# One tile of left rows for a block instead of one for a step, and dense operands turned one unit a step in the forward chain

## The chip, the cores and the metric

The kernel runs on one core of a Trainium2 chip. The time is device time of one execution in microseconds; it is given as the median of several runs. Besides these runs there is one profiled execution, from which all views of the profile come. TensorE is called PE in the profile (its weight loads PEld), VectorE DVE, ScalarE ACT, GpSimd POOL and SyncE SP. "DMA share" is the mean busy share of the core's 16 DMA engines.

## The reference

Two functions of the same layer-normed input are added to x, and the whole is differentiated: the outputs are the result and the gradients of all ten inputs for a given grad_out, 11 arrays in bf16.

```python
xn = _layernorm(x)                     # x: 1 x 2048 x 512
return x + _A_ref(xn, mem0, Wq, Wk, Wv, Wo, 32) + _B_ref(xn, w1, b1, w2, b2)

def _A_ref(...):                       # 32 heads of 128, M = 8 memory rows
    mem = mem0                         # 8 x 512
    for s in range(64):                # segments of 32 rows, one after the other
        h = concatenate([mem, xs])     # 40 rows
        q, k, v = h @ Wq, h @ Wk, h @ Wv
        scores = where(mask, q k^T * scale, -1e9)    # idx_q < 8, or causal
        o = softmax(scores) @ v @ Wo
        mem = o[:8]; outs.append(o[8:])

def _B_ref(...):                       # F = 1792
    r = relu(x @ w1 + b1)
    return r * r @ w2 + b2
```

The memory rows make the 64 segments a chain, forwards and, for the gradients, backwards. A memory row attends to all 40 keys of its segment.

## The kernel before

**Rows.** Of a segment's 40 rows (8 of memory, 32 of x) a step of the chain handles 32: the memory and the first 24 of x. They are called the main rows. The last 8 rows of a segment, the *left rows*, take no part in making the next memory as queries, but their keys and values do, and these hang on x alone. Their q, k and v are projected ahead for a whole block and kept in DRAM in S_NL[b][:, t], t = 0, 1, 2 for q, k, v. A block is four segments, j = 0 to 3, so a block has 32 left rows for each of four groups of heads: the 128 partitions are 4 groups of 32 rows, and left row m of segment j lies at row 8j + m of its group. Each group has eight heads, which stand side by side in 1024 columns (GW).

**Stages**, in order of time: the dense function B with its backward part to 215 us; the first left rows to 250; the forward chain to about 1110; its tail; the left-back stage from 1143 to about 1386 (16 iterations, one per block: the gradients of left queries, and beside them the dense weight gradients); the backward chain to about 2330 (64 steps, from the last segment to the first); the weight gradients of A (L1639) to the end.

**Order.** In both chains the instructions are issued in an order written by hand. F_ORDER and B_ORDER list names of small pieces of work in four strings, one for each step of a block ("slots"); a plus sign behind a name means one step (or, for names with "L.", one block of the left thread) later. `play` walks through it. Each engine then executes its own instructions in that order. In the backward chain slot 0 is segment j = 3, slot 3 is j = 0. Plain transfers named `dma` and all DMA transposes sit on one queue, SyncE's; it is in order, so an entry that waits holds back all behind it. `pdma` is GpSimd's queue.

**Attention in a step.** `scores` (L467) computes q k^T into PSUM, the softmax writes the probabilities to E [128, 8 heads, KW = 64 columns] (all zero at the start): columns 0 to 31 the main keys, 32 to 39 the left keys. `turn` (L480) transposes 32x32 blocks on DVE, so that for each head ET has main keys (`[.., 0, :]`) and left keys (`[.., 1, :]`) on the partitions. `outer` (L620) then multiplies, for each head and group, main values by the first and left values by the second, both into the same PSUM tile f_pp. Since the second block has only 8 rows with keys, the left values of the step must lie at partitions 0 to 7 of each group. So `left_of_step` (L636 to 639) loads them for every step by four DMAs of 16 KB, into f_vLs forwards (values, the name `ld`; two buffers) and into b_kLs backwards (keys, the name `ldk`, L1336; one buffer), where `qp` multiplies the transposed score gradients gST by them. The backward chain's further loads of a step (qN, kN, P, the transposed values vl with `vtr`) come from S_A, where the forward chain stored them (soV L956, soN L957, soP L958). The left thread of the forward chain has also a tile of a whole block's left values, VL (one buffer, loaded by L.lv), as well as vM, the memory rows' values.

**Stores of gradients.** The backward chain collects the gradients of q, k, v in G4 for a block; in slot 0 six stores of 512 KB (L1238, names L.vo1, L.vo0, L.qo0, L.ko0, L.ko1, L.qo1) take them to S_GB. The casts (evictions) `ve`, `ke` and `qe` of the next block write the same G4.

**Dense weight gradients.** They need the hidden activations and their gradients with rows on partitions, while the dense stage stored both turned: S_AT and S_GH1T, [4 row blocks, 1792, 512]. In the left-back stage `chunk` (L1085) loads 256 of the 1792 columns of one of them by four DMA transposes of 256 KB each to wB, one chunk an iteration ahead, 14 chunks; `product` (L1101, L1106) multiplies it by the other operand wA, which stays in SBUF. The iteration's other loads (transposed left values vTL, vTM, P, kM, kL) are on the same queue ahead of the chunk (`load`).

**The names in short.** f_vLs, b_kLs: a step's left values and keys. VL: a block's left values. S_AT, S_GH1T: dense operands as stored. wB: a chunk, turned. E, P, gS: probabilities and score gradients. kT, vT: transposed keys and values of a step, copied together from main and left.

Of the kernel before, what the change touches and what calls it, by code (L numbers as in the profile page):

```python
# [8 lines left out]
ALU = mybir.AluOpType  # L9
# [17 lines left out]
def kernel(  # L27
# [96 lines left out]
    S_GH1T = dram.tile([NRB, F, RB], BF16, name="S_GH1T")  # L124

# [47 lines left out]
    def masks(pool, temp):  # L173
# [11 lines left out]
        for g in range(HG):  # L185
            sl = slice(32 * g, 32 * g + 32)

            keep(maskA[sl, :, M:SEG], [[0, KM], [-1, XS]], -M, 1)
            nc.gpsimd.memset(maskA[32 * g:32 * g + M, :, :], 0.0)

            keep(maskl1[sl, 0], [[-M, SPB], [0, M]], 0, 1)
            keep(maskl1[sl, 0], [[M, SPB], [0, M]], M - 1, -1)
            keep(maskl1[sl, 1], [[-M, SPB], [-1, M]], 0, 1)
            keep(maskl1[sl, 1], [[-M, SPB], [0, M]], 0, 1)
            keep(maskl1[sl, 1], [[M, SPB], [0, M]], M - 1, -1)
# [11 lines left out]
    with sb("p1b", 2) as p1b, sb("p1", 1) as p1:  # L207
# [90 lines left out]
        for rb in range(NRB):  # L298
# [26 lines left out]
            else:  # L325
# [6 lines left out]
                XL0, X0 = (smp.tile([P, DC, P], BF16, name=n) for n in ("XL0", "X0"))  # L332
# [161 lines left out]

    C01, C23 = slice(0, 2), slice(2, 4)
# [67 lines left out]
    def ds_ops(o, p, n, sc, Pb, gS, sm):  # L563
# [14 lines left out]
        def d4():  # L578
            nc.vector.scalar_tensor_tensor(out=gS()[:, HALF[p], 0:n], in0=t[0][:], scalar=scale,  # L579
                                           in1=Pb()[:, HALF[p], :], op0=ALU.mult, op1=ALU.mult)  # L580
        o["d1%d" % p], o["d2%d" % p], o["d3%d" % p], o["d4%d" % p] = d1, d2, d3, d4

    def soft_ops(o, p, n, sc, E, st, sm, tag, pre=""):
# [21 lines left out]
        def pmf():  # L605
            e = nc.vector if ENGS[pre + "pm%d" % p] is vcp else nc.gpsimd
            e.tensor_tensor(out=E()[:, HALF[p], 0:n], in0=st[p][:], in1=bc(ss[1], n), op=ALU.mult)
# [3 lines left out]
    def outer(pp, h, jobs, base=0):  # L611

        for k in range(4):
            for i, (c0, w, ends, m, N_, X) in enumerate(jobs):
                for g in range(HG):
                    o = pp[g // 2][:, g % 2, base + k * c0:base + k * c0 + w]
                    if ends:
                        o = o.rearrange("p (a n) -> p a n", a=2)[:, :, 0:M]
# [16 lines left out]

    def left_of_step(eng, dst, b, j, t):  # L636

        for g in range(HG):
            eng(dst[32 * g:32 * g + M], S_NL[b, 32 * g + M * j:32 * g + M * j + M, t, :])
# [14 lines left out]
    def play(order, n, steps, lefts, step, blk, done=None):  # L654
# [20 lines left out]

    F_ORDER = (
# [3 lines left out]
        "ta+++ Ha+++ L.u2 L.mx0+ L.t1 soV+++ tb+++ L.X2 Hb+++",  # L680
# [5 lines left out]
        "rb+++ L.oa0+ ta+++ Ha+++ tb+++ Hb+++",  # L686
# [4 lines left out]
        "tu1+++ w1+++ L.lq++ oa1+++ ob1+++ g0+++ g1+++ soN++ ra+++ rb+++ ta+++ Ha+++ tb+++ L.otr+ Hb+++",  # L691
# [986 lines left out]
```

## Time and profile before

| what | value |
|---|---|
| runs | 2919.82, 2922.25, 2928.49 us; median 2922.25 |
| profiled execution: own time, span, granted clock | 2915.0 us, 2913.1 us, 0.971 |
| forward chain, 250 to 1110 us | 860 us, PE busy 810 |
| left-back stage, 1143 to 1386 us | 243 us, PE busy 193 |
| backward chain, 1386 to 2330 us | 944 us, PE busy 870 |
| wB transposes (L1085) in that stage | 56, four for each of 14 chunks |
| f_vLs and b_kLs loads | 256 each of 16 KB |

A stage of the profile is read from its window: the length, the busy time and number of instructions of each engine, the clock that TensorE was granted, the share of the DMA engines and the GB/s they moved. A row of waits reads "engine, its operation and line, `<-` what ended the wait", then the total in us, the number of times and the longest. A row that ends in "issue" is idle time in which the profile shows no event that the engine waited for. The granted clock is 1.00 at full speed.

### The profile page before, as it was taken

Reading aid. Unit: us, or ns where it says so; the run is one execution under the profiler, and the core shown is the slowest. Engines: PE = TensorE matmul, PEld = TensorE weight load, DVE = VectorE, ACT = ScalarE, POOL = GpSimd, SP = SyncE. Lnnn points to the kernel's source line nnn. Section 1 sums busy time; section 2 is a strip of 40 time slices with the busy share of each in tenths; the row PEclk is TensorE's granted clock in tenths of the full one; section 3 lists DMA queues with packets and bytes.
Section 4 is the critical chain, followed back from the end, with each engine's and each line's share of the span. In section 5 each row is a group of like instructions: output and inputs, shape, how many; then the busy total and the mean of one; then the engine's idle time right before and its main releaser. Section 6 shows DMA issues by size and latency. Waiting matters only on the chain.

```text
span 2913.1 us, 115280 instructions
## 1 busy us (share of the span) xinstructions
PE 2702.2 (93%) x51252; PEld 1450.9 (50%) x51252; DVE 1277.8 (44%) x3754; ACT 1001.7 (34%) x2330; POOL 660.6 (23%) x1278
## 2 busy tenths in 40 slices
PE   7997999999999887888898999999999999999999
PEld 3444555555555555355454554455555444444444
DVE  4533566666665654343454545454445401100000
ACT  2313444444444445232333333333333301111111
POOL 1000000000000001122333433343334324332221
PEclk9998999999999998998899999999999999999999
DMA  9766477667676668999666687677767799999993
GB/s 250 259 207 164 138 184 189 184 188 182 180 192 166 170 156 201 227 225 213 148 167 164 179 220 173 172 180 211 184 170 181 223 273 224 220 209 237 217 210 71
DMA packets 835429, 561.50 MB, mean 193 GB/s; under 512 B 642177, under 2 KB 727698, under 8 KB 833394
## 3 DMA queue, kind: packets, MB, share of 16 engines
q1 hardware_dynamic: 794018, 431.40, 64.6%
q0 software_dynamic: 40912, 122.73, 14.0%
q8 instruction: 402, 6.59, 0.9%
q14 instruction: 97, 0.79, 0.1%
HBM read 174.47 MB, written 234.11 MB: 140 GB/s over the span
## 4 chain that ended last, share of the span: by engine, by line
PE 42%; DMA 7%; issue 2%; DVE 1%; SPq 1%; POOL 0%; ACT 0%; ACTq 0%; DVEq 0%; POOLq 0%
PE ps_gw L1639 17%; PE ps_gR L490 11%; PE ps_proj L422 3%; PE b_pp L620 3%; PE ps_RL L1251 3%; DMA b_kLs<-S_NL 2%; PE b_T L525 1%; PE ps_tr L164 1%; DMA gn<-S_OL 1%; DMA b_qN<-S_A 1%; PE ps_R L490 1%; DMA S_GM<-b_GN 1%; PE b_pp L1383 1%; PE ps_sc L467 1%; DMA b_GN<-GT 0%
## 5 line engine op out<-in xcount | busy, mean ns | idle before, releaser
L1639 PE MATMUL ps_gw<-gn,HNc 128*128 128x512 bf16 x1920 | 416.8, 379 | 0.0
L1639 PEld LDWEIGHTS <-HNc 128*128 128x128 bf16 x1920 | 187.9, 98 | 223.6
L404 ACT CAST f_N<-ps_proj 128x512 bf16<-128x512 f32 x320 | 183.9, 581 | 199.4 <-PE ps_proj L422 192.6
L1572 ACT CAST wt<-ps_gw 128x512 bf16<-128x512 f32 x128 | 74.0, 588 | 451.3 <-PE ps_gw L1639 412.0
L422 PEld LDWEIGHTS <-X 128*32 128x32 bf16 x6144 | 152.6, 96 | 143.1 <-DVE X L534 21.9
L1555 DVE TENSOR_TENSOR gx<-ps_rows,gb 128x512 f32<-128x512 f32 x16 | 11.1, 692 | 426.4 <-PE ps_rows L1553 426.4
L895 POOL COPY kM<-f_kT 128x256 bf16<-128x256 bf16 x64 | 25.8, 403 | 736.0 <-DVE f_kT L407 562.2
L490 PE MATMUL ps_gR<-Wv,gv 128*32 128x512 bf16 x2048 | 145.0, 404 | 6.9 <-issue 6.9
L1639 PE MATMUL ps_gw<-GOc,gn 128*128 128x512 bf16 x640 | 141.0, 383 | 10.2 <-ACT wt L1572 8.7
L490 PE MATMUL ps_gR<-Wk,gk 128*32 128x512 bf16 (+1 forms) x2048 | 141.1, 387 | 1.3 <-ACT gk L404 0.8
L490 PE MATMUL ps_R<-Wo,OT 128*32 128x256 bf16 x4096 | 135.6, 289 | 1.1 <-DVE OT L407 1.1
L422 PE MATMUL ps_proj<-Wq,X 128*32 128x512 bf16 x2048 | 134.7, 380 | 0.1
L404 ACT CAST gk<-b_pp 128x256 bf16<-128x256 f32 x192 | 70.7, 379 | 184.0 <-PE b_pp L620 116.1
L422 PE MATMUL ps_proj<-Wk,X 128*32 128x512 bf16 x2048 | 130.9, 380 | 0.8
L422 PE MATMUL ps_proj<-Wv,X 128*32 128x512 bf16 x2048 | 131.3, 382 | 0.0
L404 ACT CAST gON<-ps_proj 128x512 bf16<-128x512 f32 x128 | 75.0, 586 | 157.4 <-PE ps_proj L422 157.4
L490 PE MATMUL ps_gR<-Wq,gq 128*32 128x512 bf16 (+1 forms) x2048 | 122.8, 348 | 6.8 <-issue 6.8
L422 PE MATMUL ps_proj<-Wo,GT 128*32 128x512 bf16 x2048 | 123.3, 382 | 3.7 <-DVE GT L1296 3.6
L1573 POOL DMA_DIRECT2D out_dram<-wt x120 | 65.0, 543 | 255.7 <-ACT wt L1572 241.0
L1332 POOL COPY PD<-b_P 32x320 bf16<-32x320 bf16 x256 | 115.3, 450 | 8.0
L490 PEld LDWEIGHTS <-OT 128*32 128x32 bf16 x4096 | 109.3, 102 | 9.9 <-DVE OT L407 1.3
L1327 POOL DMA_DIRECT2D b_P<-S_A x63 | 33.9, 538 | 349.9 <-DVE gS L579 115.6
(276 smaller groups left out, 5256.7 us busy)
## 6 DMA issues: line engine op xcount, KB each, us to landing
S_A<-f_N SPq DMA_DIRECT2D x64, 512.0 KB
out_dram<-wt POOLq DMA_DIRECT2D x134, 128.0 KB, 4.9
S_A<-f_N SPq DMA_DIRECT2D x64, 256.0 KB
S_GB<-gv SPq DMA_DIRECT2D x32, 512.0 KB
S_GB<-gq SPq DMA_DIRECT2D x32, 512.0 KB
S_GB<-gk SPq DMA_DIRECT2D x32, 512.0 KB
b_kN<-S_A POOLq DMA_DIRECT2D x63, 256.0 KB, 3.9
b_qN<-S_A POOLq DMA_DIRECT2D x63, 256.0 KB, 4.1
```

The lines of the kernel that those rows point to most:

```text
L164: nc.tensor.transpose(ps_ap, in_ap, ident[base:base + k, base:base + k])
L404: nc.scalar.copy(out, in_)
L422: nc.tensor.matmul(o, lhsT=hT[:, dc, :], rhs=x, start=(dc == 0), stop=(dc == DC - 1), tile_position=(0, 32 * g))
L467: nc.tensor.matmul(sc3[32 * g:32 * g + 32, k, c:c + n], lhsT=qT[:, 4 * h + k, g, :], rhs=kT[:, 4 * h + k, g, :], start=(mask is None), sto ...
L490: nc.tensor.matmul(R[32 * g:32 * g + 32, 0:(cs.stop - cs.start) * P].rearrange("p (a b) -> p a b", b=P), lhsT=XT(k, g), rhs=x[:, cs, :], s ...
L620: nc.tensor.matmul(o, lhsT=N_[32 * g:32 * g + m, kk * P:(kk + 1) * P], rhs=X(kk)[32 * g:32 * g + m], start=(i == 0), stop=(i == len(jobs) ...
L1251: nc.tensor.matmul(ps["R", i][32 * g:32 * g + 32, :].rearrange("p (a b) -> p a b", b=P), lhsT=B_[n][:, k, g, :], rhs=W(g * KH + k), start= ...
L1327: q(tile_of("P", [P, KH, KW])[:], rows[:, 3 * GW:AC].rearrange("p (k n) -> p k n", k=KH))
L1332: nc.gpsimd.tensor_copy(PD[32 * g:32 * g + 32, g], C["P"][32 * g:32 * g + 32, :, 0:L])
L1572: nc.scalar.copy(wt[:], ps[:])
L1573: eng(dst, wt[:])
L1639: nc.tensor.matmul(ps[:], lhsT=l(rc), rhs=r(rc), start=(n == 0), stop=(n == RC_ALL - 1))
```

## The change

1. *Order of rows.* In kT, vT, in E, P and gS and in all that is evicted from products with them, the 8 left rows come first (columns 0 to 7) and the main rows after (`MAIN = slice(8, 40)`). E and gS use the last columns of their 64: left 24 to 31, main 32 to 63; 0 to 23 stay zero. Masks, score operands and products are swapped to match.
2. *Left rows of a block in one tile.* `turn` gets j and reads overlapping windows of E: for every head 32 columns that start at 24 - 8j, and 32 that start at 32. So the left keys of segment j come to rows 8j to 8j + 7, with zeros before them, and `outer` multiplies rows 0 to 8 + 8j of the block's tile. Forwards that tile is VL, now with two buffers and loaded in slot 0 one block ahead. Backwards it is a new tile kNL (one buffer), loaded once a block in two halves of 128 KB, ldk1 and ldk0, on SyncE's queue in slot 0. f_vLs, b_kLs and `left_of_step` are gone.
3. *Dense operands turned ahead.* In steps 4 to 59 of the forward chain each step transposes one unit of 256 KB (`aw`, a DMA transpose to the tile `box`, which uses the space of XL0 and X0) and stores it plainly (`as`) to the new DRAM arrays S_AN and S_GH1N, both on SyncE's queue. `chunk` in the left-back stage is then one plain load of 1 MB.
4. *Orders.* F_ORDER and B_ORDER are cut in other places between slots, which alone moves nothing on PE, DVE and ACT: the sequence of their operations is the one before, but for which of the two operands of a product comes first. On SyncE's queue, in a block of the forward chain, four `aw` and four `as` come in, soP of one step is behind VL, and 16 loads of f_vLs go. In the backward chain 16 loads of b_kLs go, and ldk1 stands ahead of L.vo1, ldk0 ahead of L.vo0. `first` puts the first chunk on GpSimd's queue.

```diff
-    def turn(ET, E, h):
-        nc.vector.transpose(ET[:].rearrange("p k a q -> p (k a q)"),
-                            E[:, HALF[h], :].rearrange("p k n -> p (k n)"))
+    def turn(ET, E, h, j=None):
+        ...
+            x = E[:, HALF[h], XS - M * j:]
+            nc.vector.transpose(ET[:].rearrange("p k a q -> p (k a q)"),
+                                bass.AP(x.tensor, x.offset, [x.ap[0], [KW, 4], [M + M * j, 2], [1, SEG]]))
...
-            e.tensor_tensor(out=E()[:, HALF[p], 0:n], in0=st[p][:], in1=bc(ss[1], n), op=ALU.mult)
+            e.tensor_tensor(out=E()[:, HALF[p], KW - n:KW], in0=st[p][:], in1=bc(ss[1], n), op=ALU.mult)
...
-    def left_of_step(eng, dst, b, j, t):
-        for g in range(HG):
-            eng(dst[32 * g:32 * g + M], S_NL[b, 32 * g + M * j:32 * g + M * j + M, t, :])
...
-                          "VL": (fo, [P, GW], BF16), "vM": (fo, [P, GW], BF16), "EL": (fo, [P, KH, KW], BF16),
+                          "VL": (fs, [P, GW], BF16), "vM": (fo, [P, GW], BF16), "EL": (fo, [P, KH, KW], BF16),
...
-                                          (32, 32, False, M, vLs[s], lambda k: st["ET%d" % p][:, k % 4, 1, :])))
+                                          (32, 32, False, M + M * j, B_["VL"], lambda k: st["ET%d" % p][:, k % 4, 0, :])))
...
+            if 0 <= s - U0 < len(units):
+                srcT, dstN, n_, rb_ = units[s - U0]
+                o["aw"] = lambda: nc.sync.dma_start_transpose(BOX, srcT[rb_][n_ * 2 * P:(n_ + 1) * 2 * P, :])
+                o["as"] = lambda: dma(dstN[n_][:, rb_ * RCB:(rb_ + 1) * RCB, :], BOX)
...
-        def chunk(b):
+        def chunk(b, eng=dma):
...
-            for rb in range(NRB):
-                nc.sync.dma_start_transpose(part[b][:, rb * RCB:(rb + 1) * RCB],
-                                            (S_GH1T if second else S_AT)[rb][n * CH:(n + 1) * CH, :])
+            eng(part[b][:], (S_GH1N if second else S_AN)[n])
...
-        "o0mm++++ pb+++ o1mm++++ L.vo1+ L.qst o0ev++++ L.vo0+ xa+++ L.xt L.qo0+ o1ev++++ o0fl++++ xb+++ L.ra0+ "
+        "o0mm++++ pb+++ o1mm++++ ldk1+++ L.vo1+ L.qst o0ev++++ ldk0+++ L.vo0+ xa+++ L.xt L.qo0+ o1ev++++ o0fl++++ "
...
-            o["ldk"] = lambda: left_of_step(dma, tile_of("kLs", [P, GW])[:], b, j, 1)
+            for p in range(2):
+                o["ldk%d" % p] = lambda p=p: dma(B_["kNL"][:, HC[p]], S_NL[b][:, 1, HC[p]]) if j == SPB - 1 else None
...
-                                     (32, 32, False, M, C["kLs"], lambda k: st[p][:, k % 4, 1, :])), 4 * KW)
+                                     (32, 32, False, M + M * j, B_["kNL"], lambda k: st[p][:, k % 4, 0, :])), 4 * KW)
```

More of the change, by code (lines that the diff above doesn't have):

```diff
@@ L124 @@
     S_GH1T = dram.tile([NRB, F, RB], BF16, name="S_GH1T")
+    S_AN = dram.tile([F // (2 * P), P, TC, 2 * P], BF16, name="S_AN")
+    S_GH1N = dram.tile([F // (2 * P), P, TC, 2 * P], BF16, name="S_GH1N")
     AC = 3 * GW + KH * KW
@@ L331 @@
                 smp = sm_cm.__enter__()
-                XL0, X0 = (smp.tile([P, DC, P], BF16, name=n) for n in ("XL0", "X0"))
+                box = smp.tile([P, 2, DC, P], BF16, name="box")
+                XL0, X0 = box[:, 0], box[:, 1]
                 nc.gpsimd.tensor_copy(XL0[:], first["XLa"][:])
@@ L876, in fwd @@
             ps, st, o = {}, {}, {}
[L878 to L888 removed]
             def ld0():
                 turned_rows(B_["kL"][:], 0, 1)
[L892 removed]
+                dma(B_["VL"][:], S_NL[0][:, 2, :])
             o["ld0"] = ld0
[L894 to L895 removed]
+            o["kl"] = lambda: nc.gpsimd.tensor_copy(T["kT"][:, :, :, 0:M], B_["kL"][:, :, :, lc])
+            o["km"] = lambda: nc.gpsimd.tensor_copy(B_["kM"][:, :, :, lc], T["kT"][:, :, :, M:2 * M])
             for t, u, n in ((1, 2, "k"), (0, 1, "q"), (2, 0, "v")):
@@ L959, in fwd @@
             return o
-        vLs = {}
+        BOX = box[:].rearrange("p x c r -> p (x c r)").rearrange("p (a f) -> p a f", f=2 * P)
+        units = [(a, b, n, rb) for a, b in ((S_AT, S_AN), (S_GH1T, S_GH1N)) for n in range(F // (2 * P)) for rb in range(NRB)]
+        assert RCB * 2 * P == 2 * DC * P and U0 + len(units) <= NSEG
         TURNS = [(Wqkv[t], n) for t in (1, 0, 2) for n in range(HD * DC // (8 * P))]
@@ L1020, in lback @@
             o["ld"] = ld
-            o["first"] = lambda: (load(i_, nc.gpsimd), chunk(i_ + 1))
+            o["first"] = lambda: (load(i_, nc.gpsimd), chunk(i_ + 1, pdma))
             for i in range(2):
@@ L1471 @@
             first["ldn"](dma)
-            first["ldk"]()
+            first["ldk0"]()
+            first["ldk1"]()
             ldk(NB - 1, dma)
             for s in range(1, NSEG):
-                for n in ("vtr", "vc", "ldp", "pb", "ldq", "ldn", "ldk"):
+                for n in ("vtr", "vc", "ldp", "pb", "ldq", "ldn", "ldk0", "ldk1"):
                     steps[NSEG - s][n] = steps[NSEG - 1 - s][n]
-            for n in ("vtr", "vc", "ldp", "pb", "ldq", "ldn", "ldk"):
+            for n in ("vtr", "vc", "ldp", "pb", "ldq", "ldn", "ldk0", "ldk1"):
                 steps[0][n] = lambda: None
```

97 lines of the change are left out of this document (46 added, 51 removed), and 65 rows, old and new, of tables (B_ORDER, F_ORDER).

## The prediction

> **What bounds the kernel now.** I read the page first, then a table of stages, then the waits of the three stages that the change touches.
>
> ```profile
> span 2913.1 us, 115280 instructions
> PE 2702.2 (93%) x51252; PEld 1450.9 (50%) x51252; DVE 1277.8 (44%) x3754; ACT 1001.7 (34%) x2330; POOL 660.6 (23%) x1278
> ...
> q1 hardware_dynamic: 794018, 431.40, 64.6%
> ```
>
> PE is busy 93% of the span, so a change that takes no matmul away can only win idle PE time or clock. The stages (forward chain; left-back stage; backward chain), with PE, PEld, DVE, ACT and POOL busy, granted clock, DMA share, GB/s:
>
> ```profile
> 250.00:1110.00 860.00, 810.35 (x20534) 469.25 (x20534) 531.57 (x1668) 406.12 (x926) 52.68 (x130) 0.97 0.67 174
> ...
> 1165.00:1263.00 98.00, 83.09 (x1415) 37.48 (x1413) 35.94 (x83) 24.63 (x56) 16.70 (x31) 0.97 1.04 220
> 1263.00:1280.00 17.00, 10.79 (x268) 8.39 (x265) 8.45 (x17) 9.90 (x15) 4.93 (x8) 0.87 0.99 260
> 1280.00:1375.00 95.00, 80.85 (x1585) 59.40 (x1584) 37.27 (x87) 23.47 (x54) 26.31 (x50) 0.93 1.01 218
> ...
> 1386.00:2330.00 944.00, 869.77 (x22729) 471.80 (x22731) 460.20 (x1447) 357.21 (x973) 361.79 (x698) 0.97 0.72 182
> ```
>
> The left-back stage is the one where the DMA engines are full (shares 0.99 to 1.04) while PE idles; yet they move only 220 GB/s there. In both chains PE works 92 to 94% of the time and the DMA has about 30% free. Who makes PE wait, in the left-back stage and then in the backward chain (sum, times, longest):
>
> ```profile
> PE ps_w L1101 <- DMA wB<-S_AT: 14.7, 13, 2.5
> ...
> PE ps_w L1106 <- DMA wB<-S_GH1T: 12.2, 12, 2.3
> ...
> PE ps_sc L467 <- DMA l_vTL<-S_NL: 6.7, 1, 6.7
> ```
> ```profile
> ACT gk L404 <- DMA S_GB<-gk: 19.9, 8, 4.2
> ...
> PE b_pp L620 <- DMA b_kLs<-S_NL: 14.5, 16, 4.8
> ```
>
> 27 us are the turned chunks of the dense weight gradients, 14.5 us the small loads of left rows. In the forward chain PE waits for no such transfer worth a line: the matching row (f_vLs) has 2.5 us, on the weight load. SyncE's own waits in the backward chain, and one of the forward chain:
>
> ```profile
> SPq L639 <- PE b_pp L620: 71.1, 16, 7.7
> ```
> ```profile
> SPq L958 <- DVE E L607: 65.8, 32, 8.6
> ```
>
> **Part 1, left-back stage: chunks come already turned.** Fourteen iterations load 1 MB each as four transposes of 256 KB. One costs, in DMA time: the backward burst of plain stores (1852 to 1866) runs 362 GB/s at share 1.10, so 329 GB/s for all engines; an iteration here is 14 us at 1.04, 14.6 us of all engines, and moves 3.08 MB. Of that 1.31 MB are transposes (four of wB, one of a left tile); the other 1.77 MB at 329 take 5.4 us, so a transpose takes 9.2/5 = 1.83 us (estimate) against 0.8 plain. The new iteration needs 14.6 - 4 x 1.83 + 3.2 = 10.4 us of DMA. PE's need is 83.09/7 = 11.9 and 80.85/7 = 11.6 us, so PE becomes the bound. The waits of 27.0 us go; the lost clock of 98 x 0.03 + 95 x 0.07 = 9.6 us may go in part. The DMA still fills 0.9 of an iteration, so something of other loads' waits comes back. What is late next is the evictions between two products. The first waits (6.7 us) and the ramp at 1263 stay. I take -28, bounds -37 (all clock back) and -10 (the waits only shrink, since every iteration keeps 10.4 us of transfers with the load behind others on SyncE). POOL issues only the first chunk, 1 MB; its other loads wait less than one issue (0.5 us).
>
> The Trainium skill ("Advanced Engine Details and Errata", section X-Bar Transpose) says that transposing DMAs are as fast as regular ones, 350 to 400 GB/s. By it the 1 MB would cost the same either way, and this part would win nothing: the trace's 220 GB/s at a full share speaks against it.
>
> **Part 2, backward chain: one left tile a block.** Gone: 256 loads of 16 KB, four a step, 0.3 us of issue each when free, 134 us of SyncE's 552 busy. Added: 32 loads of 128 KB, two a block. The rows on PE cost the same whatever the depth: the 8-row matmul lasts 175 ns, the 32-row one 172 to 177. So 8 to 32 rows instead of 8 are free, bound 0 to 2 ns x 2048 = 4 us. The turn on DVE now reads overlapping windows; contiguous it takes 441 ns, and a strided 128x256 cast takes 423, so 0, bound +0.2 us x 128 of which PE, whose qp reads gST, would see a quarter: up to +6. Narrower outputs (16 in one run, not 2 x 8) stay at 164 ns.
>
> The waits: PE steps of a block last 17.2, 13.1, 13.1, 15.9 us. The last (slot 3) has 14.0 at best; of its excess of 16 x 1.9 = 30 us, 11.3 us are 11 waits for b_kLs, and the clock after one falls too: around 1847 PE waits 1.9 us, and then
>
> ```profile
> 1846.00:1848.00 2.00, 0.64 (x7) 0.27 (x3) 0.94 (x3) 0.00 (x0) 0.83 (x1) 1.00 0.45 104
> 1848.00:1850.00 2.00, 1.41 (x42) 0.74 (x45) 0.00 (x0) 0.95 (x4) 2.00 (x6) 0.78 0.69 123
> 1850.00:1854.00 4.00, 4.00 (x102) 1.62 (x98) 0.56 (x2) 0.25 (x1) 2.06 (x4) 0.69 0.83 239
> ```
>
> that is 2 x 0.22 + 4 x 0.31 = 1.7 us lost to the clock behind 1.9 us of waiting. So slot 3 gives back about 20 us: 11.3 of waits and some 9 of clock (six long waits at 1.5). The Trainium skill ("TensorE: Matmul & The Clock Gate", section HAM oscillation) says that the clock halves only after an idle window of about 3.4 us. By it 1.9 us would cost no clock and this slot would give 11 us; the rows above show a clock below full behind a shorter gap, and decide.
>
> Against it: the single tile has one buffer. Its first half (ldk1) waits in SyncE's queue until the old block's last qp1 has ended, and it stands ahead of the stores of the block's gradients (vo1, vo0, then qo, ko: S_GB, six of 512 KB). Before, vo1 went out some 2.6 us ahead of that moment, and afterwards it can go 0.45 us behind it: the burst starts 1 to 5 us later, about 3. Its readers are the evictions into G4, which already wait 19.9 + 3.5 us for these stores; in 6 to 8 blocks of 16 there is no slack. So 7 x 2.5 = 17 us more waiting on ACT, of which PE sees about a third now (6.0 us of its gaps against 23.4), about half when it grows: +8, bounds 0 and 16 x 2.5 = +40. The slot-0 waits for b_kLs (3.2 us) go. And 134 us of SyncE issue are freed, worth a microsecond or two at the b_qN waits. Sum -20 - 3 + 8 + 4 (DVE, instruction gaps) = about **-11**, bounds -35 and +25.
>
> **Part 3, forward chain: the units are turned here.** Per step, 56 times, SyncE gets one transpose and one 256 KB store, and loses four 16 KB loads (104 us of issue in all, 0.4 each). An issue of a transpose takes 1.3 to 1.8 us, a store 0.4 to 0.5: 56 x 2.1 = 118 us added, 104 removed. SyncE is busy 576 of 860 us and waits on compute for the rest, so the stores and loads behind it keep nearly their places; the E store (soP) goes behind the VL load once a block. A store out of the box also waits for the transpose, and the next transpose for the store: 2 to 4 us each, with SyncE standing; about 12 us of its waiting in a block of 53.7 can be spent on that. DMA: 0.67 x 860 = 576 us, + 56 x (1.83 + 0.8) - 12 = 711, share 0.83, so queues fill more often than now but not throughout. Cover that hides it: PE's chain, with no wait for a transfer now; if it goes (SyncE late by 1 us a step at the feed of E and N stores) every late us of a step is paid, 56 us. I take **+6** (instruction fetches behind fuller DMA: adding up the time in which neither PE nor PEld works and nothing releases it, the backward chain at 0.72 has 37 us, this one 7), bounds -3 (the 2.5 us of f_vLs) and +35.
>
> DVE's 128 turns here: 0, bound +6 as above. The renamed columns of E, P, masks and evictions move nothing: same sizes, same order on ACT and DVE.
>
> **Sum.** -28 - 11 + 6 = -33 against the profiled execution's 2915.0, that is 2882. The median of the runs is 2922.25, 7 above it, so **2889**.
>
> **Rivals.**
> (a) The burst of the backward chain is the price: ldk1 ahead of vo1 makes every block's G4 evictions 2.5 us late on PE. For it: no slack in half the blocks, the DMA at 1.10 there. Against: the last of the six stores (ko1) goes out only 2.6 us later, by the queue's order 5.1 us behind qp1 where it is 2.5 now. It decides from 2 us a block on. Backward +25 in place of -11: 2922 - 28 + 25 + 6 = 2925, no change.
> (b) Slower: SyncE runs late in the forward chain. Each step has a chain transpose, landing, store, landing on one in-order queue, and behind it the transposes and stores that feed the left stage. If they cost PE 1.1 us a step (from 0.7 us on, all that the other parts win is gone: 39/56), forward +62: 2922 - 28 - 11 + 62 = 2945. For it: SyncE busy 67% plus such waits, DMA to 0.83. Against: 240 us of SyncE's time there are waits on compute, and the removed loads pay the new issues.
> (c) Left-back stays bound by the DMA, or by the loads' queue: -6 there; 2922 - 6 - 11 + 6 = 2911. The Trainium skill's rule above would make this one. Against: 1.83 us against 0.8.
> (d) Everything goes, with the clock: -37 - 30 + 0 = 2855.
>
> **How the numbers follow.** Mine 0.46, (d) 0.12, (a) 0.17, (b) 0.17, (c) 0.08. Less than 0.3% (9 us) can't be told from no change. Faster than 2913: mine, (d), half of (c) and a third of (a): 0.67. Same (2913 to 2931): the other half of (c), a third of (a), a little of (b): 0.12. Slower: the rest, 0.21. The range takes in (d) and nearly all but the far side of (b): 2855 to 2942. Mine alone is 2870 to 2908.
>
> **What would show it.** Left-back stage: waits for wB below 5 us, 16 iterations of 12 us, shares near 0.9, stage shorter by 25 to 30. Backward: no row b_kLs in chain or waits, slot 3 near 14.6 us; the row of gk's evictions on S_GB near 30 us; a row kNL on PE would be a new wait. Forward: still 13.4 us a step, share 0.83, no PE wait for VL. Wrong if forward steps with a unit differ from the first four and last four by over 0.5 us, if the turn on DVE is over 0.6 us, or if PE waits for kNL.

## The result and the profile after

The change makes the kernel slower: 2940.3 us median of 16 runs (2919.0 to 2959.3) against 2918.1 us of 16 runs of the kernel before (2899.3 to 2933.8), a ratio of 1.0088 with a 95% interval of 1.0067 to 1.0109. The forecast was 2889 us and faster. The time lies inside the stated range, at its far end, and the sign is wrong.

The profiled execution after has a span of 2936.0 us, 22.9 more than before. To place them, four borders were read from both traces: the first and the last product f_pp of a step (the forward chain) and the first and the last score product from b_vT (the backward chain). What lies between them is the tail with the left-back stage.

| stage, us | before | after | difference | forecast |
|---|---|---|---|---|
| start to the forward chain | 263.9 | 267.9 | +4.0 | 0 |
| forward chain | 843.0 | 883.8 | +40.8 | +6 |
| tail and left-back stage | 278.3 | 249.0 | -29.3 | -28 |
| backward chain | 928.7 | 937.7 | +9.0 | -11 |
| weight gradients, to the end | 599.2 | 597.7 | -1.5 | 0 |

The +4.0 is scatter: a second profile of the kernel before starts its forward chain at 270.3 us, a second one of the changed kernel at 263.2.

The stage table of the profile after (length; PE, PEld, DVE, ACT, POOL busy; clock; DMA share; GB/s), for the forward chain, the left-back stage and the backward chain, and under it the left-back stage of the kernel before:

```profile
268.00:1152.00 884.00, 809.14 (x20375) 470.33 (x20420) 527.37 (x1655) 400.14 (x917) 51.52 (x127) 0.97 0.81 194
...
1200.00:1401.00 201.00, 175.82 (x3520) 112.45 (x3542) 89.69 (x203) 64.74 (x136) 52.62 (x97) 0.96 0.93 246
1401.00:2338.00 937.00, 858.33 (x22424) 464.46 (x22424) 453.15 (x1426) 353.49 (x962) 355.07 (x689) 0.96 0.73 178
```
```profile
1147.00:1385.00 238.00, 188.63 (x3527) 113.77 (x3525) 90.22 (x204) 65.36 (x136) 52.61 (x97) 0.91 1.02 219
```

PE does the same work in each stage as before; in the forward chain 74.9 of 884 us are without a product, against 40.9 of 843 before (802.15 busy). The chunks' waits in the left-back stage have shrunk from 27 us to these:

```profile
PE ps_w L1104 <- DMA wB<-S_GH1N: 2.9, 2, 2.1
...
PE ps_w L1099 <- DMA wB<-S_AN: 1.8, 1, 1.8
```

What the forward chain waits for is in its table of waits, before and after:

```profile
PE f_pp L620 <- ACT OT L404: 3.4, 6, 0.9
...
PE f_pp L620 <- DMA vM<-S_A: 0.6, 2, 0.3
```
```profile
PE f_pp L629 <- ACT OT L407: 22.8, 16, 3.1
...
ACT OT L407 <- issue: 22.1, 7, 5.1
...
PE f_pp L629 <- DMA vM<-S_A: 6.8, 9, 2.0
```

PE waits for casts into OT, and those casts wait for something that the profile doesn't name. The waits of SyncE's queue in the same stage point at it, first before and then after:

```profile
SPq L758 <- DMA S_ON<-OC: 74.4, 33, 4.8
```
```profile
SPq L762 <- DMA S_ON<-OC: 102.4, 43, 4.2
...
SPq L950 <- DMA box<-S_AT: 27.4, 14, 3.7
SPq L950 <- DMA box<-S_GH1T: 19.2, 14, 2.8
```

L762 (L758 before) is the transpose of OT into the tile OC. OC has one buffer, which a transpose and a store of the left rows (ON) share. Each block transposes four quarters of OT through it (t3, t2, t1, t0) and stores each (u3 to u0), so a transpose must wait for the store before it to land. OT has two buffers, and a block may write its OT only when t0 of the block two before is through. One block in time, SyncE's queue (start, duration), and ACT beside it:

```profile
537.02 1.63 SPq L770 DMA_DIRECT2D S_ON<-OC  x1
538.71 0.42 SPq L950 DMA_DIRECT2D S_AN<-box  x1
539.18 0.45 SPq L955 DMA_DIRECT2D S_A<-f_N  x1
541.43 2.08 SPq L762 DMA_TRANSPOSE OC<-OT  x1
543.55 2.81 SPq L643 DMA_DIRECT2D vM<-S_A  x4
546.41 1.24 SPq L949 DMA_TRANSPOSE box<-S_AT  x1
```
```profile
544.96 0.65 ACT L407 CAST OT<-f_pp 128x256 bf16<-128x256 f32 x2 [2.47 <-issue]
```

The store u1 leaves at 537.0, t0 stands until 541.4, and OT's cast, which has stood for 2.47 us, starts at 544.96; vM, queued behind t0, starts 2.1 us behind t0. Averaged over twelve blocks, t0 is issued 47.5 us into a block before the change and 54.1 after (from a block's first product f_pp; the steps' own lengthening is in that). Measured from one step's first product f_pp to the next one's, slot 0 of a block lasts 16.0 us against 13.9 before, slot 3 14.0 against 13.5, the other two the same within 0.2: nearly all of the loss stands in the slot in which a block first writes its OT.

In the backward chain the waits for b_kLs are gone, and new ones stand at the evictions into G4 (first the row of gv before, then after; that of gk was 19.9 us):

```profile
ACT gv L404 <- DMA S_GB<-gv: 3.5, 4, 1.3
```
```profile
ACT gk L407 <- DMA S_GB<-gk: 31.0, 15, 3.6
ACT gv L407 <- DMA S_GB<-gv: 28.5, 9, 4.7
...
PE b_pp L629 <- ACT b_gvL L407: 23.3, 10, 3.5
```

From one step's first product with Wo to the next one's, the steps of a block last 19.4, 13.1, 13.0 and 14.2 us against 17.2, 13.1, 13.1 and 15.9 before: slot 3 gained 1.7 us, slot 0 lost 2.2.

### The profile page after: what moved, and what is told of

It reads as the page before. It is cut to its first block, busy times and chain, and to the rows that moved or that the text cites. A ratio compares the mean times of both kernels' runs of the same rounds, so it can differ in the third digit from the quotient of the medians.

```text
span 2936.0 us, 114536 instructions
## 1 busy us (share of the span) xinstructions
PE 2696.1 (92%) x51115; PEld 1454.1 (50%) x51252; DVE 1277.2 (44%) x3754; ACT 1002.0 (34%) x2330; POOL 660.1 (22%) x1279
## 3 DMA queue, kind: packets, MB, share of 16 engines
q0 software_dynamic: 41056, 123.77, 14.4%
## 4 chain that ended last, share of the span: by engine, by line
PE 71%; DMA 13%; SPq 5%; DVE 5%; issue 3%; ACT 2%; POOL 0%; another core or an unknown queue 0%; ACTq 0%; DVEq 0%; POOLq 0%
PE ps_gw L1638 15%; PE ps_proj L425 13%; PE ps_gR L498 11%; PE ps_R L498 4%; PE b_pp L629 3%; DMA S_GB<-gk 3%; PE ps_tr L166 2%; PE ps_RL L1248 2%; PE ps_L L383 2%; PE ps_sc L470 2%; PE ps_B L344 2%; PE f_pp L629 1%; PE ps_w L1104 1%; PE ps_gxb L353 1%; PE f_T L534 1%
## 5 line engine op out<-in xcount | busy, mean ns | idle before, releaser
L425 PEld LDWEIGHTS <-X 128*32 128x32 bf16 x5760 | 144.0, 96 | 136.0 <-DVE X L543 20.9
L498 PE MATMUL ps_gR<-Wv,gv 128*32 128x512 bf16 x2048 | 152.1, 421 | 0.8 <-issue 0.8
L425 PE MATMUL ps_proj<-Wq,X 128*32 128x512 bf16 x1920 | 127.1, 380 | 2.5 <-DVE dN L410 2.5
L425 PE MATMUL ps_proj<-Wk,X 128*32 128x512 bf16 x1920 | 125.0, 381 | 0.8
L425 PE MATMUL ps_proj<-Wv,X 128*32 128x512 bf16 x1920 | 121.4, 378 | 0.0
```

What stands on the lines that cost most here:

```text
L425: nc.tensor.matmul(o, lhsT=hT[:, dc, :], rhs=x, start=(dc == 0), stop=(dc == DC - 1), tile_position=(0, 32 * g))
L498: nc.tensor.matmul(R[32 * g:32 * g + 32, 0:(cs.stop - cs.start) * P].rearrange("p (a b) -> p a b", b=P), lhsT=XT(k, g), rhs=x[:, cs, :], s ...
```

## The experiments

Each kernel ran beside the kernel before on its chip; ratios are to that. Medians of different chips aren't compared: e12 and e13 are one kernel, with 2897.0 and 2912.0 us on chips where the kernel before has 2906.8 and 2918.0. Stage times are from the one profiled execution of each kernel, by the borders above. The executions scatter: two profiles of the kernel before give 843.0 and 845.1 us forwards, 928.7 and 920.2 backwards; two of the changed kernel 883.8 and 882.6, 937.7 and 946.0. A single profile of the backward chain thus tells nothing below some 10 us. In the forward chain unchanged code gave 867.0 (e3) as well as 883.8, so there it tells nothing below some 15 us. The totals of single runs lie up to 10 to 30 us from their median.

| kernel | ratio (95%) | forward | tail, left-back | backward |
|---|---|---|---|---|
| changed, again (e10) | 1.0073 (1.0043 to 1.0103) | 882.6 | 251.0 | 946.0 |
| no units (e1) | 1.0060 (1.0040 to 1.0081) | 846.6 | 275.7 | 938.4 |
| one unit moved (e2) | 1.0063 (1.0040 to 1.0087) | 875.2 | 250.1 | 938.4 |
| ldk behind vo0 (e3) | 1.0054 (1.0027 to 1.0082) | 867.0 | 247.5 | 928.0 |
| both moves (e4) | 1.0029 (1.0009 to 1.0050) | 863.5 | 248.1 | 920.2 |
| both, stores and vM on GpSimd (e5) | 1.0110 (1.0078 to 1.0142) | 860.0 | 245.6 | 942.0 |
| both, units' transposes alone (e6) | 0.9957 (0.9929 to 0.9985) | 852.0 | 244.2 | 932.9 |
| both, units' stores alone (e7) | 0.9958 (0.9925 to 0.9991) | 856.3 | 247.0 | 930.5 |
| both, OC twice (e8) | 0.9953 (0.9925 to 0.9982) | 855.3 | 247.5 | 934.3 |
| unit moved, OC twice, old left keys (e9) | 0.9945 (0.9919 to 0.9970) | 852.6 | 241.9 | 927.0 |
| both, OC twice, no q stores (e11) | 0.9931 (0.9897 to 0.9965) | 851.9 | 248.0 | 923.8 |
| OC twice alone (e12) | 0.9974 (0.9955 to 0.9994) | 849.3 | 247.9 | 927.9 |
| OC twice alone, again (e13) | 0.9969 (0.9945 to 0.9994) | 851.3 | 247.8 | 946.6 |
| OC twice, ldk behind vo0 (e14) | 0.9941 (0.9917 to 0.9966) | 858.1 | 247.7 | 938.8 |
| OC twice, old left keys (e15) | 0.9907 (0.9873 to 0.9941) | 844.0 | 247.0 | 932.7 |
| before, again (e16) | 1.0002 (0.9973 to 1.0030) | 845.1 | 280.7 | 920.2 |

### e1: without the units

```diff
-            if 0 <= s - U0 < len(units):
+            if False:
...
-            eng(part[b][:], (S_GH1N if second else S_AN)[n])
+            for rb in range(NRB):
+                nc.sync.dma_start_transpose(part[b][:, rb * RCB:(rb + 1) * RCB],
+                                            (S_GH1T if second else S_AT)[rb][n * CH:(n + 1) * CH, :])
```

> The changed kernel without its third part: the forward chain turns no dense units, the left-back stage turns its chunks itself as before. Theory 1 (the units on SyncE's queue cost the forward chain its 41 us): the forward chain goes from 884 back to 843 to 850 us, the left-back stage from 201 back to about 238, the backward chain stays at 937; total about 10 us above before, 2925 to 2935. Theory 2 (the overlapping turn on DVE and the block's tile of left values cost the forward chain): the forward chain stays at 875 to 884 and the total is about 2965.

The forward chain falls to 846.6 us and the left-back stage goes back up to 275.7. So the units, and not the overlapping turn or the block's tile, cost the forward chain its time. The same run prices the third part where it pays: 249.0 against 275.7, 26.7 us, for chunks that come turned. The kernel without units is still slower than the one before, by 0.6% (17 us), where about 10 us were expected: its backward chain is that of the change, with 938.4 us.

### e2, e3, e4: two places in SyncE's queue

e2 moves the unit of slot 0: its transpose from behind soN, where u2 and t1 come next, to behind soP, and its store to behind soN. e3 moves ldk behind vo0. e4 does both.

```diff
-        "... s1+++ L.u3 v0mm+++ mx1+++ ex0+++ soP++ su0+++ sb1+++ ... L.lp ob1+++ soN++ aw oa1+++ g1+++ ..."
+        "... s1+++ L.u3 v0mm+++ mx1+++ ex0+++ soP++ aw su0+++ sb1+++ ... L.lp ob1+++ soN++ as oa1+++ g1+++ ..."
...
-        "q0fl+++ xb++ L.u1 k0fl+++ k1fl+++ q1fl+++ q0Te+++ k0Te+++ as- soN++ s0+++ ..."
+        "q0fl+++ xb++ L.u1 k0fl+++ k1fl+++ q1fl+++ q0Te+++ k0Te+++ soN++ s0+++ ..."
```
```diff
-        "o0mm++++ pb+++ o1mm++++ ldk1+++ L.vo1+ L.qst o0ev++++ ldk0+++ L.vo0+ xa+++ L.xt L.qo0+ ..."
+        "o0mm++++ pb+++ o1mm++++ L.vo1+ L.qst o0ev++++ L.vo0+ xa+++ L.xt ldk1+++ ldk0+++ L.qo0+ ..."
```

> The changed kernel with one unit of the four of a block moved on SyncE's queue: the transpose from behind soN (ahead of the store u2 that the next transposes of OT wait for) to behind soP, where the queue waits for u3's landing anyway, and its store from slot 1 to behind soN. Same number of bytes and transfers. Theory 1 (place in the queue: u2, t1, u1, t0, vM run late behind this unit, and OT's release and vM with them): the forward chain goes from 884 to 852 to 864 us, total 2910 to 2920. Theory 2 (the DMA's share of 0.81 makes every transfer late, wherever the unit stands): the forward chain stays at 876 to 888, total 2930 to 2942.

> The changed kernel with ldk1 and ldk0 behind vo1, qst and vo0 on SyncE's queue, directly ahead of qo0, which waits for the evictions after qp1 anyway. Theory 1 (ldk1 waits for the old block's qp1 and holds vo1 and vo0, so the evictions of v and k wait): slot 0 goes from 19.4 to about 17 us, waits of gv's evictions on S_GB from 28 to below 8 us, the backward chain from 937 to 900 to 908, total 2905 to 2912. Theory 2 (the burst of stores itself, or the loads of kNL in it, is what slot 0 pays for): slot 0 stays above 18.5 us, total 2930 to 2942.

> Both moves together. If both queue theories hold and add: forward chain 852 to 864, backward chain 900 to 908, total 2875 to 2890, clearly faster than before (2918). If only one holds: 2905 to 2920. If neither: 2935 to 2942.

The moved unit gives 875.2 us in e2 and 863.5 in e4, the forward code of the change 883.8, 882.6 and, in e3, 867.0. The two overlap, so a gain by the place of one unit isn't shown; theory 1 of e2, in the form that this place is the cause, has no support. In e3 the waits for gv's evictions are gone (b_gvL 17.4 us of PE's gaps, the time in which neither a product nor a weight load runs, before the move, none after), as theory 1 said, but the chain is 928.0 and not 900 to 908, and slot 0 is 18.2 us. The sizes of both expectations were too large; e4 misses its 2875 to 2890 with a median of 2913.0, where one theory alone was expected to bring it, and the medians of e2 (2926.5) and e3 (2922.5) lie between their two theories.

### e5, e6, e7: another queue, and the two halves of a unit

e5 issues the units' stores and vM from GpSimd's queue, on top of e4. e6 leaves out the stores, e7 the transposes.

```diff
-                o["as"] = lambda: dma(dstN[n_][:, rb_ * RCB:(rb_ + 1) * RCB, :], BOX)
+                o["as"] = lambda: pdma(dstN[n_][:, rb_ * RCB:(rb_ + 1) * RCB, :], BOX)
...
-            o["lm"] = lambda: memory_rows(B_["vM"], b, 0)
+            o["lm"] = lambda: memory_rows(B_["vM"], b, 0, nc.gpsimd)
```

> The kernel with both moves, and beside them the stores of the units (as) and the loads of the memory rows' values (vM) issued from GpSimd's queue, which is busy 52 of 850 us in the forward chain. Same transfers, same bytes; SyncE loses some 2.8 + 4 x 0.45 us of issue a block and its waits for the transposes' landing. Theory 1 (SyncE's in-order queue is late: at t0 it stands 4 to 5 us later in the block than before the change): forward chain 846 to 855 us, no wait of PE for vM or of ACT's OT, total 2885 to 2897. Theory 2 (the DMA engines at 0.81 make every link of the chain t, u, t, u land late): forward chain 860 to 870 as with both moves, total 2900 to 2913.

> The kernel with both moves, without the stores of the turned units (left out: the arrays of turned operands are never written, and the left-back stage multiplies the unturned ones, so two weight gradients are not computed). What is left of the third part is 56 transposes on SyncE. Theory 1, queue: of the units' 20 us in the forward chain the issue and waits of the transposes (1.45 us each and no wait for landing any more) remain, forward chain 848 to 856. Theory 2, DMA time: the transposes are 1.8 of 2.6 us a unit, forward chain 857 to 864.

> The kernel with both moves, without the transposes of the units (left out: the stores write what the tile happens to hold, so two weight gradients are not computed). 56 plain stores of 256 KB remain on SyncE, 0.45 us of issue each. Theory 1, queue: nothing waits for a landing, forward chain 844 to 850. Theory 2, DMA time: 0.8 of 2.6 us a unit, forward chain 848 to 853. Here the two hardly differ; together with the transposes alone the two must add to what both cost.

With vM on another queue PE's wait for it falls from 6.4 us to 1.3, but the wait for OT's casts stays (row f_pp on OT: 13.0 us against 15.1), and so does the forward chain (860.0 against 863.5): relieving SyncE of these issues is not enough. Either half of the units alone costs about half (852.0 and 856.3). The theories stay undecided: e5's chain is where theory 2 had it, e6's where theory 1 had it, and e7's is above both. Why e5's total is worse than e4's by 0.8% isn't settled: its profiled execution has 942.0 us backwards and 617.6 in the weight gradients against 920.2 and 607.5, in code that is the same.

### e8, e12: a second buffer for OC

One number, in the two places that make the tile, with both moves (e8) and on the changed kernel alone (e12):

```diff
-                        st["OC", g] = fo.tile([P, KH, P], BF16, name="OC", tag="OC", bufs=1)
+                        st["OC", g] = fo.tile([P, KH, P], BF16, name="OC", tag="OC", bufs=2)
...
-                st["ON"] = fo.tile([P, KH, P], BF16, name="ON", tag="OC", bufs=1)
+                st["ON"] = fo.tile([P, KH, P], BF16, name="ON", tag="OC", bufs=2)
```

> The kernel with both moves, with a second buffer for OC, so that a transpose of OT no longer waits for the store of the one before it to land (the waits of 102 us at L762 on SyncE). Theory 1 (the chain t3, u3, t2, u2, t1, u1, t0 on one buffer, stretched by the units, lets OT go and vM in late): PE's wait for ACT's OT and for vM goes, forward chain from 863 to 846 to 853, total 2890 to 2900. Theory 2 (the DMA engines' time): forward chain stays at 857 to 866.

> The changed kernel with nothing but a second buffer for OC: all units and ldk where the change put them. Theory 1 (the chain on OC's one buffer is what the units stretch in the forward chain, and the place of one unit hardly matters): forward chain 852 to 860, backward chain 934 to 946, total 0.998 to 1.002 of before. Theory 2 (the moved unit is needed as well): forward chain 864 to 875, total 1.003 to 1.007 of before.

The forward chain of e12 is 849.3 us with every unit in the place that the change gave it, 34.5 below the changed kernel and 6.3 above the kernel before, and the kernel is now 0.3% faster than before, in e12 and again in e13. The 34.5 us are from two profiles. The forward code of the change has three (883.8, 882.6, and 867.0 in e3: mean 877.8) and that of e12 has four (849.3, 851.3, 858.1, 844.0 in e12 to e15: mean 850.7): the groups don't overlap, and by their means the one buffer costs 27 us. e12 is below the 852 to 860 that theory 1 had, and e8, at 855.3, lies between its two theories. The row of e12's forward chain in the stage table and the waits that answer to those above:

```profile
263.00:1112.00 849.00, 800.46 (x20392) 462.83 (x20380) 526.62 (x1654) 399.87 (x916) 51.53 (x127) 0.98 0.86 202
```
```profile
PE f_pp L629 <- ACT OT L407: 4.0, 6, 1.0
...
PE f_pp L629 <- DMA vM<-S_A: 0.6, 1, 0.6
```

The DMA share is higher than after the change (0.86 against 0.81), with the same bytes in less time, and these waits of PE are back at the size that they had before. So full DMA engines (theory 2) are not the cause: what the units did was to lengthen a serial chain through one tile. Whether its links grew by what stands ahead of them in the queue or by landing later is not separated by these runs. On SyncE the row of t waiting for u (102.4 us) is gone; its two largest rows are now waits for compute:

```profile
SPq L954 <- ACT f_N L407: 61.6, 22, 12.3
SPq L956 <- DVE E L616: 43.7, 22, 9.7
```

And t0 goes out 45.8 us into the block, earlier than before the change. The size of the row alone would not have told: it is 74.4 us before the change and 96.2 in e1, whose forward chain loses nothing clear of the scatter and whose t0 goes out at 47.5, as before. What counts is whether the chain's end, t0, is late for OT.

The kernel before was not run with a second buffer. There PE waits 3.4 us for OT's casts and 0.6 for vM, so its rows show little to win.

### e9, e11: the backward chain, first try

e9 takes e8 and loads the left keys of each step as before (with j = 0 in the turn, so that they lie in rows 0 to 7). e11 takes e8 and leaves out the two stores of q's gradients.

```diff
-                                     (32, 32, False, M + M * j, B_["kNL"], lambda k: st[p][:, k % 4, 0, :])), 4 * KW)
+                                     (32, 32, False, M, C["kLs"], lambda k: st[p][:, k % 4, 0, :])), 4 * KW)
```
```diff
-                        dma(S_GB[b, t][:, gs, ks], G4[n][:, gs, ks].rearrange("p g k j r -> p g k (j r)"))
+                        if n != "q":
+                            dma(S_GB[b, t][:, gs, ks], G4[n][:, gs, ks].rearrange("p g k j r -> p g k (j r)"))
```

> As the kernel with both moves and two buffers of OC, but with the backward chain's left keys loaded for each step as before the change (second part undone there only, row order kept). Theory 1 (one tile a block is a gain backwards once ldk stands behind vo0): backward chain 925 to 932, 5 to 10 us longer than with kNL. Theory 2 (slot 0 is bound by the burst of S_GB stores, and what slot 3 wins waits there): backward chain 922 to 930, no difference beyond 5 us in the total.

> The kernel with both moves and two buffers of OC, without the two 512 KB stores of q's gradients a block (left out: the gradient of Wq is made from k's gradients instead). 1 MB less in the burst of slot 0, about 3 us of all DMA engines a block. Theory 1 (slots 3 and 0 of the backward chain are bound together by the burst of S_GB stores and the loads in it, 33.0 to 34.0 us in every version, so what slot 3 wins is waited for in slot 0): slots 0 and 3 together go from 33.4 to 30.5 to 32 us, the backward chain from 934 to 890 to 912. Theory 2 (slot 0's gaps have another cause, instruction fetch or the order of the evictions): 33 to 33.6, the backward chain 925 to 935.

e9's backward chain is shorter than e8's by 7.3 us in the profiles, where theory 1 wanted it longer; the totals are equal within their intervals, as theory 2 had it. In e11 the stores' absence takes PE's wait for gk's casts from 10.4 to 1.0 us, yet slot 0 stays at 18.4; slot 3 falls from 15.0 to 14.4. Slots 0 and 3 together are 32.8 us, outside both theories (30.5 to 32, and 33 to 33.6). PE's gaps, those of 0.25 us and more, fall from 71.4 to 61.1 us in the whole chain; those that end in issue are 36.7 us of them, against 41.9 in e8, while those on the loads of b_qN grow from 4.3 to 8.7. A burst shorter by 1 MB did not free slot 0.

### e10, e13 to e16: three backward chains on one forward chain

> The changed kernel itself on the chip of the other two, for comparison with them and as a second profile of it. All theories: 1.006 to 1.011 of before; forward chain 870 to 885, backward chain 934 to 941, tail and left-back stage 247 to 251.

> The changed kernel with a second buffer for OC once more, on the chip of the next three, as their base: one left tile a block backwards, ldk1 and ldk0 ahead of vo1 and vo0. All theories: 0.995 to 1.000 of before, forward chain 848 to 858, backward chain 926 to 942.

> The base with ldk1 and ldk0 behind vo0. Theory 1 (the loads' wait for qp1 costs the backward chain because the S_GB stores start late): the evictions' waits on S_GB (b_gvL, gv, gk in PE's gaps, about 30 us in the base) fall to about 10, and the total is 8 to 15 us below the base. Theory 2 (whatever is late in slot 0, something else waits there as long): the evictions' waits fall in the same way, but the backward chain and the total stay within 5 us of the base, with more idle PE time on loads and instruction fetch.

> The base with the left keys loaded backwards for each step as before the change. Theory 1 (the tile's waits for qp1 are the loss): 5 to 12 us below the base, as in the kernel with ldk late. Theory 2: within 5 us of the base; the 15 to 20 us of waits for b_kLs are back in slot 3, and slot 0 is shorter by as much.

> The kernel before once more, for a second profile of its stages on this chip. All theories: 0.998 to 1.002 of before; forward chain 840 to 848, tail and left-back stage 275 to 280, backward chain 922 to 932.

e13, e14 and e15 have the forward chain of e12 and differ in the backward chain alone: ldk where the change has it, ldk behind vo0, and the old loads of each step. The medians are 2912.0, 2901.1 and 2892.7 us. So the early ldk costs about 11 us by the medians (8 by the ratios), as theory 1 said. The old loads are 19 below the base, where theory 1 had 5 to 12: the tile costs something even with ldk late. Only these 19 us are clear of the intervals; those of e13 and e14 overlap a little. The second step, 8 us, is less sure still: the intervals of e14 and e15 overlap, and e8 and e9, the same pair with the unit moved, differ by 3 us. The profiled backward chains don't order the three kinds by themselves: e12 and e13, one kernel, have 927.9 and 946.6 us, and e10, e12, e13 and e16 lie 2 to 6 us outside the bands expected for them. The waits on S_GB and b_kLs in e13, in e14 (where gv has none) and in e15:

```profile
ACT gv L407 <- DMA S_GB<-gv: 34.6, 9, 7.6
ACT gk L407 <- DMA S_GB<-gk: 32.9, 15, 3.7
```
```profile
ACT gk L407 <- DMA S_GB<-gk: 26.0, 9, 3.9
...
PE b_pp L1383 <- DMA b_gOL<-S_GOL: 6.5, 4, 3.0
```
```profile
ACT gk L407 <- DMA S_GB<-gk: 21.0, 9, 3.4
...
PEld L629 <- DMA b_kLs<-S_NL: 18.2, 22, 2.5
```

The mean lengths of the two slots over all profiles, by kind of backward chain (4 kernels with loads per step, 6 with the tile and ldk early, 7 with ldk late):

| backward chain | slot 3 | slot 0 | both | whole chain |
|---|---|---|---|---|
| loads per step (before, e16, e9, e15) | 16.07 | 16.93 | 33.0 | 927.2 |
| one tile, ldk early (after, e1, e2, e10, e12, e13) | 14.29 | 19.39 | 33.7 | 939.2 |
| one tile, ldk late (e3 to e8 and e14) | 14.84 | 18.39 | 33.2 | 932.4 |

Slot 3 wins 1.8 us a step by the tile, 28 us in all, and slot 0 gives 2.5 back, 39 us. With ldk late, slot 3 wins 1.2 and slot 0 gives back 1.5. What slot 0 waits for in the tile's place isn't one thing, and PE's gaps over the whole chain show an exchange. With ldk early, the gaps behind the casts that wait for S_GB are 25.9 to 35.2 us in all six profiles and those that end in issue 18.5 to 22.2. With ldk late, the first are 8.8 to 12.5 in all seven and the second 35.0 to 53.6, with up to 10.7 us on loads of the left stage (gOL). With loads per step they are 3.0 to 6.5 and 21.0 to 33.6. So moving ldk takes away some 20 us of one and brings about as much of the other. Slots 3 and 0 together stay at 32.5 to 34.2 us in these 17 profiles, and the means of the kinds differ by 0.7 us at most, 11 us over 16 blocks. What sets that sum stays open. It isn't the bytes of q's stores to S_GB (e11).

e15, which keeps the first and third part, the block's tile forwards and the second buffer, is the fastest: 2892.7 us, 0.9907 of before (0.9873 to 0.9941) in six runs. It beats both kernels.

## Why the prediction was wrong

**Left-back stage: right in the cause and the size, not in how the size is made up.** Forecast -28, measured -29.3, and -26.7 by the comparison with e1. The two prices, 1.83 us of all DMA engines for a transposed unit against 0.8 plain, were sound: the stage's length times its DMA share falls from 243 to 187 us, about 1.0 us for each of 56 units, the DMA share fell to 0.93 (0.9 forecast) and the waits for wB to 4.7 us (below 5). But PE's idle time in the tail and the stage fell by only 16 us, since other waits grew. The other 13 us are PE's products, which take 210 us instead of 223 with the clock at 0.96 instead of 0.91 in the stage. That the total met the forecast so closely is partly luck. The Trainium skill ("Advanced Engine Details and Errata", section X-Bar Transpose) says that transposing DMAs are as fast as regular ones; by that rule plain chunks would have won nothing here. The 26.7 us that they won against e1 disagree, and decide.

**Forward chain: wrong, +40.8 for +6; this is the step that turns the sign.** The failing sentence is that the stores and loads behind the units keep nearly their places, since SyncE waits on compute for the rest of its time. It added up slack on a queue: 104 us of issue removed against 118 added, 12 us of waiting in a block to spend. But part of SyncE's waiting wasn't on compute: of the 240 us that the prediction called waits on compute, the rows of that stage show 209, and 88 more on transfers. 74.4 us of these, in 33 waits, are L758 on the store S_ON<-OC, which the prediction did not show. That is a serial chain of eight transfers a block through one tile, with a deadline at OT's second buffer. A unit ahead of a link lengthens that link, and there are several in a block: t0 went out at 54.1 us of a block instead of 47.5. The sum of free time on the queue said nothing on this. e12 gives the price of the chain, 34.5 us forwards for one buffer (27 by the means of all profiles of the two forward codes). What is left over the kernel before, 6.3 us (6.6 by the means), agrees with the +6 that the prediction gave to the units themselves, as far as profiles tell that scatter by 14 us. The sign that was to show a slow forward chain, steps with a unit longer than those without by over 0.5 us, did not show it: they last 14.0 us in the mean, the first four 13.8 and the last four 13.6, since the loss stands in one step of four. Rival (b) had the sign and half as much again (+62 at 1.1 us a step; measured 0.73 over 56 steps), with the wrong chain: it blamed the box's transposes and stores, and what waited was OC's. That its total, 2945, is so near is luck: it had 21 us too much forwards and 20 too little backwards.

**Backward chain: both terms mis-sized.** Slot 3 did give back what was forecast and more, -27 us for -20 (15.91 to 14.23 us a step). The term for ldk ahead of vo1 was +8 with a bound of +40; slot 0 took +35 (17.19 to 19.37). PE's gaps behind the casts that wait for S_GB grew from 6 to 30 us, so they are 24 of these 35. The delay itself was as described: SyncE's queue after the change issues ldk1 at 1865.60, and vo1 directly behind it.

```profile
1865.60 0.33 SPq L1334 DMA_DIRECT2D b_kNL<-S_NL  x1
1865.97 0.43 SPq L1235 DMA_DIRECT2D S_GB<-gv  x1
...
1867.61 1.58 SPq L1235 DMA_DIRECT2D S_GB<-gv  x1
```

That PE sees about half of these waits held (30 of 31.0 + 28.5 us on ACT, against 6 of 23.4 before). What was too small is their growth: 17 us forecast, 36 measured, in 15 blocks where 6 to 8 were expected to have no slack. That is the mechanism of rival (a), at less than half its price: +25 forecast for the chain, +9 measured in one profile and +12 in the mean of the kinds. The prediction also took for granted that slot 3's gain stays won; the means of both slots over all versions show that most of it comes back in slot 0 even with ldk late.

**Right where it cost at nothing.** The turn on overlapping windows takes 445 and 440 ns (bound +0.2 us); the products with 8, 16, 24 or 32 rows all 171 ns:

```profile
L488 DVE STREAM_TRANSPOSE ET<-E x128: 445/445/448, 267.3 to 1150.8; 128x256 bf16<-128x256 bf16 x128
L488 DVE STREAM_TRANSPOSE gST<-gS x128: 428/440/448, 1403.2 to 2340.7; 128x256 bf16<-128x256 bf16 x128
```

The forward chain's DMA share was forecast at 0.83: 0.81 in the stretched chain and 0.86 in e12. No row of waits has PE waiting for VL or for kNL.

## What to carry to other kernels

Before putting more transfers on an in-order queue, look in its waits for a transfer that waits for another transfer on the same tile: such a chain has a deadline of its own, and idle time on the queue says nothing about it. The size of that wait doesn't say how near the deadline is (here 74.4 and 96.2 us cost nothing clear of the scatter, and 102.4 did); the time at which the last link goes out, against the time at which its buffer is needed, does. A second buffer there (one number here) may be worth more than any choice of place. And a wait that is removed from one step of a loop is only won if nothing else takes its place in the next; here slot 3 won 28 us and slot 0 gave back 39.

## What was not expected of the hardware

Gaps of PE that end in issue are, in the backward chain, by their times mostly gaps of instruction supply. The kernel before has 28 of more than 0.25 us there, 33.6 us together. In 24 of them, and in all 12 that last over 1 us, a packet of the instruction queue (q8) had landed 1.2 to 1.6 us before the gap ended; with 175 such packets in 929 us, chance would give this for 7.5% of the gaps. In the 18 profiles these gaps add up to 18.5 to 53.6 us in that chain, at DMA shares of about 0.72, and to 7.2 to 18.2 us in the forward chain, at shares of 0.65 to 0.87. So the mean share doesn't order the two chains. Within the forward chain the kernel before has the least (7.2 and 8.8), and e1, without units and with the lowest share, has 12.3. The Trainium skill ("Runtime: NRT & Kernel Launch", section Instruction fetch mechanics) says that the cost of crossing into the next block of instructions is mostly hidden; here some is not. What makes a packet late wasn't tried.

The 9 us of lost clock that the prediction counted behind the waits for b_kLs can't be separated by any run: the backward chain's granted clock is 0.96 after and 0.97 before. The 1.9 us of waiting near 1847 us, behind which it shows a clock below full, are two waits, of 1.3 and 0.6 us.
